# Two token chunks interleaved on the arriving weights, and a gate by half the angle

## The chip, the cores and the metric

The kernel runs on one core of a Trainium2 chip. The metric is the device time of one execution in microseconds (us); the time shown is the median over runs. Five engines work side by side, each through its own list of instructions in a fixed order, and meet at semaphores: PE (TensorE, matrix products and transposes; its weight loads are shown apart as PEld), DVE (VectorE), ACT (ScalarE, with lookup tables for functions), POOL (GpSimd) and SP (SyncE, which here only issues DMAs).

## The reference

```python
scores = q @ k.T / sqrt(64)                       # batch 4, 8 heads, 768 tokens, 64 per head
keep = (column < n_sink) | ((0 <= row - column) & (row - column < window))    # 4 and 128
a = softmax(where(keep, scores, -1e9))
x = (a @ v) laid out as 3072 tokens x 512         # the heads side by side
h = x @ w_in                                      # 512 -> 2048
g = h * cos(h)
return g @ w_out                                  # 2048 -> 512
```

q, k and v come as 32-bit numbers, w_in and w_out as 64-bit numbers. The result has to hold 32-bit accuracy, so that a product of two 32-bit matrices is made of three passes of a faster matmul over a rounded part (hi) and its rest (lo): hi x hi, hi x lo, lo x hi.

## The kernel before

**Tiling.** The 3072 tokens are 12 chunks of 256. A chunk has eight heads of attention and then eight slots of the dense layer; a slot is 256 of the 2048 columns. In a slot PE makes 24 matmuls of 256 columns for h (`h_mm`, L391) and 12 of 512 columns that add g·w_out to the chunk's two accumulators (`out_mm`, L439). The three batches' first chunks come first: chunks 0, 1 and 2 are the first 256 tokens of batches 0, 1 and 2, with exact 32-bit matmuls in their heads (tiles named early, scores at L771); chunks 3 to 11 are the rest (scores at L827, from the split keys r1 of L812 and r2 of L818).

**The gate.** Between h and g of a slot, on tiles of 128 partitions x 512: ACT turns h into whole turns (`turns`, L400), DVE takes the rest of the turn (`rest`, L406), ACT looks up the sine (`cosine`, L413), DVE multiplies by h (`gate`, L418), ACT rounds g (`g_hi`, L424), DVE or POOL takes what the rounding left (`g_lo`, L430).

**The weights.** They come as 32 pieces of 512 KB, which SP loads into two buffers (raw). DVE assembles a 32-bit number out of the two halves of each 64-bit one in three passes (L499, L505, L511), ACT rounds it (L532), DVE or POOL takes the rest (L535). All 32 are converted while chunk 0 goes through its eight slots, and then stay in memory. From chunk 2 on each piece is loaded once more and looked over for numbers that are too small (`check_piece`, L550); where one is found, a branch at the end goes through the whole work again by a general path.

**Order.** A planner goes through all steps with a due time each (`head_time`, `slot_time`) and a cost, and writes a fixed order for every engine before anything is emitted; the numbers of the table `C` are its costs and due times. In it the heads of chunk 0 come first, `TH` apart; the slots of chunk 0 follow, `STEP` apart, with the heads of chunks 1 and 2 between them; from chunk 1 on a slot comes every `T`, and the heads of a chunk run about a chunk ahead of its slots. At the start PE is also given `FILL` = 120 matmuls on a tile of zeros whose result nobody reads (L1281).

**Places that the change touches.** Out copies (L380 on ACT, L382 on DVE) bring an accumulator into a raw buffer, from where SP stores it (L455). A chunk's x is split into x.hi and x.lo (L335, L352), two buffers each. The banks of the accumulators' memory (PSUM) have tags: b0 to b4, s, tp, av.

Of the kernel before, what the change touches and what calls it, by code (L numbers as in the profile page):

```python
# [26 lines left out]
C = {  # L27
    "ALT": 3.247, "BLF": 0.145, "CK": 63.541, "DA": -2.188, "DH": -1.258, "DM": -0.843, "DQ": 1.633, "DS": -3.217,
    "DV": 4.887, "DX": 6.133, "FILL": 120, "CL": 6.506, "GHI": 2, "GLO": 2, "L": 1, "LAG": 4.747, "LEAD": 22.987,
    "NEH": 24, "NM": 1.13, "NW": 0.46, "NWF": 0.209, "PB": 5, "PEN": 11.444, "POOLF": 1.457, "POOLPEN": 2.675, "R": 2,  # L30
    "RAW": 2, "SAME": 0.151, "SEM": 0.193, "SPE": 0.272, "STEP": 6.281, "T": 6.493, "TH": 3.647, "WARM": 5,
    "WARM2": 0, "P0": 10.087, "A0": -0.05, "D0": 9.99, "G0": 1.871, "S0": 1.917, "ZV": 33.968, "LD": -14.202,
    "HOT": 7.314, "RL": 4.633, "K0": -93.629, "K2": 8.334, "WI": -21.701, "WO": 0.716, "WS": -2.103, "WS2": 2.887,
    "WT": 2, "XV": 2,
}
MIN_TOP = 1.125 * 2.0**-15
# [134 lines left out]
def attn_moe_kernel(ctx, tc, q, k, v, n_sink, window, w_in, w_out, out):  # L171
# [52 lines left out]
    lims = cp.tile([1, 2, 2, 2], F32, name="lims")  # L224
    tiny = cp.tile([P, NC * NSLOT // 2 + NFT], F32, name="tiny")
    redo = cp.tile([1, 1], I32, name="redo")

    def setup():
# [15 lines left out]
        nc.scalar.activation(out=tiny[:, 0:1], in_=quarter, func=AF.Exp)  # L244
        nc.vector.memset(lims, 0.0)
# [99 lines left out]
    def x_lo(x, a, p, early):  # L345
        def fn(e):
            if p == 0:
                x.lo = xp.tile([P, NP, NT], F32R, name=f"xlo_{a}", tag="xlo", bufs=2)
            if early:
                copy(e, x.lo[:, p, :], x.f[p])  # L350
            else:
                e.tensor_tensor(out=x.lo[:, p, :], in0=x.f[p], in1=f32(x.hi)[:, p, :], op=ALU.subtract)  # L352
        return fn

    def split_x(plan, x, a, p, t, early=False):

        add, buf = plan.add, plan.buf
        if p == 0:
            x.bhi, x.blo = buf("xhi", 2), buf("xlo", 2)
        i = add(  # L360
            [("ACT", act(NT, not early))], x_hi(x, a, p), x.sums[p] + (x.firsts[:1] if x.parts else [x.bhi]), t
# [53 lines left out]

    def gate(o):
# [28 lines left out]
    def out_copy(x, a, j):  # L445
        def fn(e):
            x.o[j] = f32(raws[x.bo[j].nth]).rearrange("p n w -> p (n w)")[:, :DM]
            copy(e, x.o[j], x.acc[j])
# [93 lines left out]
    def check_piece(plan, prio, k, src):  # L542

        add, buf = plan.add, plan.buf
        r, bt = buf("raw", C["RAW"]), buf("wt", C["WT"])
        raw, t32 = raws[r.nth], f32(wts[bt.nth])
        top = raw[:, :, 1].bitcast(F32)

        def least(e):
            nc.vector.tensor_tensor_reduce(  # L550
                out=t32, in0=top, in1=top, op0=ALU.mult, op1=ALU.max, scale=-1.0, scalar=-3.0e38,
# [4 lines left out]
        j = add((("DVE", dve(WP) + 0.02),), least, [i, bt], prio, port=True)  # L556
        r.users += [i, j]
        bt.users.append(j)
        return j

    def dense(plan, x, a, s, t, T, w_in_ready, w_out_ready, acc_banks, h_bank):
# [7 lines left out]
        accs = x.bacc  # L569
        if True:  # L570
            o = Rec()
            o.s, o.m, o.bank = s, a * NSLOT + s, h_bank
            bh, by, br, bhi, blo = buf(h_bank, 1), buf("y", 1), buf("r", C["R"]), buf("ghi", C["GHI"]), buf("glo", C["GLO"])
# [10 lines left out]
            a0 = add([("ACT", act(FG * NT, False))], turns(o), mm + [by], t + C["DM"] + 7.2)  # L584
            a2 = add([("DVE", dve(FG * NT))], rest(o), [a0, br], t + C["DM"] + 8.0)
            by.users.append(a2)
            a3 = add([("ACT", act(FG * NT) + 0.09)], cosine(o), [a2], t + C["DM"] + 8.9, table="sin")
            a4 = add([("DVE", dve(FG * NT))], gate(o), [a3], t + C["DM"] + 9.5)
            bh.users += [a0, a2, a4]
# [13 lines left out]
        for j in range(CB):  # L603
            bo = x.bo[j] = buf("raw", C["RAW"])
# [12 lines left out]
    def banded_path(ctx2):  # L617
# [111 lines left out]
        def pe_turn(o, part, tile, n):  # L729
            def fn(e):  # L730
                if part == 0:
                    o.qk = ps.tile([P, 2, NT], F32, name=f"qk_{o.tag}", tag="b3")
# [76 lines left out]
        def k_hi(o):  # L809
            def fn(e):  # L810
                o.r1 = ap.tile([P, o.nkb, o.sw], F32R, name=f"r1_{o.tag}", tag="r1")
# [3 lines left out]
        def k_lo(o):  # L815
            def fn(e):
                o.r2 = ap.tile([P, o.nkb, o.sw], F32R, name=f"r2_{o.tag}", tag="r2")
# [99 lines left out]
        def sink_turn(o):  # L917
            def fn(e):
                o.gp = ps.tile([GR, NT], F32, name=f"gp_{o.tag}", tag="av")
# [74 lines left out]
        def values(o):  # L994


            def fn(e):
                o.av = ps.tile([P, NT], F32, name=f"av_{o.tag}", tag="av")
# [57 lines left out]
        def before_softmax(g, o):  # L1056
# [91 lines left out]
            o.nq = 4 if o.a else 2  # L1148
# [48 lines left out]
        def after_softmax(g, o):  # L1197
# [45 lines left out]
            bav = buf("av", 1)  # L1243
# [309 lines left out]
```

## Time and profile before

| | |
|---|---|
| runs | 731.9, 733.47, 733.95 us; median 733.47 |
| profiled execution | 733.03 us |
| its span, from the first to the last instruction | 731.3 us |
| granted clock of PE, mean | 0.998 of 2.4 GHz |
| busy share of the span | PE 98%, DVE 84%, ACT 74%, POOL 23% |

The busy share of PE counts a matmul from its start to the end of its results, and neighbours overlap: where matmuls follow one another without a wait, the next starts long before the one before has ended. So PE can be shown as 98% busy and still do less than it could. How much work went through is read from the steps between starts, not from the busy time. The fills of L1281 count as busy too.

### The profile page before, as it was taken

Reading aid. Unit: us, or ns where it says so; the run is one execution under the profiler, and the core shown is the slowest. Engines: PE = TensorE matmul, PEld = TensorE weight load, DVE = VectorE, ACT = ScalarE, POOL = GpSimd, SP = SyncE. Lnnn points to the kernel's source line nnn. Section 1 sums busy time; section 2 is a strip of 40 time slices with the busy share of each in tenths; the row PEclk is TensorE's granted clock in tenths of the full one; section 3 lists DMA queues with packets and bytes.
Section 4 is the critical chain, followed back from the end, with each engine's and each line's share of the span. In section 5 each row is a group of like instructions: output and inputs, shape, how many; then the busy total and the mean of one; then the engine's idle time right before and its main releaser. Section 6 shows DMA issues by size and latency. Waiting matters only on the chain.

```text
span 731.3 us, 15326 instructions
## 1 busy us (share of the span) xinstructions
PE 715.8 (98%) x4865; PEld 651.3 (89%) x4865; DVE 614.5 (84%) x1811; ACT 541.2 (74%) x1354; POOL 165.8 (23%) x256
## 2 busy tenths in 40 slices
PE   8999999999999999999999999999999999999996
PEld 8887889899999999989898898999988999999995
DVE  6889999878999999899989988888898888875431
ACT  3878885987778868768778687788888697774332
POOL 1010100002242232433433324323110232321000
PEclk9999999999999999999999999999999999999999
DMA  6766564331673555646365443223333132110000
GB/s 174 199 183 185 166 173 136 83 55 32 139 193 55 121 134 128 158 118 170 78 159 149 89 99 58 49 69 55 55 73 64 30 83 52 34 45 3 28 2 34
DMA packets 215519, 71.51 MB, mean 98 GB/s; under 512 B 204164, under 2 KB 204164, under 8 KB 215428
## 3 DMA queue, kind: packets, MB, share of 16 engines
q1 hardware_dynamic: 215136, 69.38, 39.7%
q10 hardware_dynamic: 292, 1.05, 0.4%
q8 instruction: 41, 0.67, 0.4%
q14 instruction: 50, 0.41, 0.2%
HBM read 64.09 MB, written 6.29 MB: 96 GB/s over the span
## 4 chain that ended last, share of the span: by engine, by line
PE 71%; DVE 14%; ACT 7%; DMA 5%; issue 2%; SPq 1%; DVEq 0%; ACTq 0%
PE acc L439 28%; PE h L391 27%; PE av L1013 5%; PE s L827 4%; PE tp L937 2%; ACT p L858 2%; DVE wt L505 2%; DVE wt L511 1%; DMA xk<-in_k_dram 1%; PE idle L1281 1%; DMA raw<-in_moe_w_in_dram 1%; DVE r L406 1%; DVE p L849 1%; DVE glo L430 1%; DVE wt L499 1%
## 5 line engine op out<-in xcount | busy, mean ns | idle before, releaser
L391 PE MATMUL h<-xhi,whi_in 128*128 128x256 f32 x768 | 226.2, 295 | 0.7 <-DVE r L418 0.5
L391 PE MATMUL h<-xlo,whi_in 128*128 128x256 f32 x768 | 216.5, 282 | 0.0
L391 PE MATMUL h<-xhi,wlo_in 128*128 128x256 f32 x768 | 216.2, 282 | 0.0
L439 PE MATMUL acc<-whi_out,ghi 128*128 128x512 f32 x384 | 154.0, 401 | 0.2 <-DVE raw L382 0.2
L391 PEld LDWEIGHTS h<-xhi,whi_in 128*128 128x128 f32 x768 | 145.3, 189 | 8.5 <-DVE r L418 1.1
L439 PE MATMUL acc<-wlo_out,ghi 128*128 128x512 f32 x384 | 151.4, 394 | 0.0
L391 PEld LDWEIGHTS h<-xhi,wlo_in 128*128 128x128 f32 x768 | 145.5, 189 | 6.0
L439 PE MATMUL acc<-whi_out,glo 128*128 128x512 f32 x384 | 150.4, 392 | 0.0
L391 PEld LDWEIGHTS h<-xlo,whi_in 128*128 128x128 f32 x768 | 145.0, 189 | 0.0
L972 POOL TENSOR_SCALAR_AFFINE_SELECT ph<-ph 128x512 fp32r<-128x512 f32 x128 | 91.3, 714 | 112.4 <-DVE ph L965 95.5
L413 ACT ACTIVATE r<-r,neg 128x512 f32<-128x512 f32 x96 | 69.3, 724 | 45.4 <-DVE r L406 44.8
L430 DVE TENSOR_TENSOR glo<-r,ghi 128x512 fp32r<-128x512 f32 x92 | 67.8, 737 | 24.2 <-ACT ghi L424 23.5
L439 PEld LDWEIGHTS acc<-whi_out,glo 128*128 128x128 f32 x384 | 72.2, 188 | 16.3
L858 ACT ACTIVATE p<-p,st 128x136 f32<-128x136 f32 (+1 forms) x192 | 79.8, 417 | 0.4
L418 DVE TENSOR_TENSOR r<-h,r 128x512 f32<-128x512 f32 x96 | 65.5, 683 | 14.9 <-ACT r L413 14.8
L439 PEld LDWEIGHTS acc<-whi_out,ghi 128*128 128x128 f32 x384 | 72.5, 189 | 5.3 <-DVE raw L382 0.4
L439 PEld LDWEIGHTS acc<-wlo_out,ghi 128*128 128x128 f32 x384 | 72.8, 190 | 4.7 <-DVE wlo_out L535 0.3
L400 ACT ACTIVATE yt<-h 128x512 int32<-128x512 f32 x96 | 57.0, 594 | 23.6 <-PE h L391 23.1
L849 DVE CUSTOM_DVE_ANT_0 p<-s,mk 128x136 f32<-128x136 f32 (+1 forms) x192 | 59.2, 309 | 11.1 <-PE s L827 4.2
L406 DVE SCALAR_TENSOR_TENSOR r<-h,yt 128x512 f32<-128x512 f32 x96 | 65.2, 679 | 3.5 <-ACT yt L400 2.5
L424 ACT CAST ghi<-r 128x512 fp32r<-128x512 f32 x96 | 59.0, 614 | 11.0 <-PE acc L439 10.5
L878 POOL TENSOR_SCALAR p<-p,st 128x136 f32<-128x136 f32 (+2 forms) x38 | 20.7, 554 | 185.8 <-DVE st L868 108.4
(131 smaller groups left out, 1320.9 us busy)
## 6 DMA issues: line engine op xcount, KB each, us to landing
raw<-in_moe_w_out_dram SPq DMA_DIRECT2D x32, 512.0 KB
raw<-in_moe_w_in_dram SPq DMA_DIRECT2D x30, 512.0 KB
xk<-in_k_dram SPq DMA_DIRECT2D x256, 48.0 KB
v<-in_v_dram SPq DMA_DIRECT2D x64, 96.0 KB
out_dram<-raw SPq DMA_DIRECT2D x24, 256.0 KB
xq<-in_q_dram SPq DMA_DIRECT2D x144, 32.0 KB
xq<-in_q_dram SPq DMA_DIRECT2D x24, 64.0 KB
xk<-in_k_dram SPq DMA_DIRECT2D x24, 64.0 KB
```

The lines of the kernel that those rows point to most:

```text
L391: nc.tensor.matmul(out=o.h[:, t, :], lhsT=w[:, c, fs], rhs=xx[:, c, :], start=(c == 0 and n == 0), stop=(c == NC - 1 and n == 2),)
L400: nc.scalar.activation(out=yt, in_=o.h, func=AF.Copy, scale=INV2PI, bias=0.25)
L406: nc.vector.scalar_tensor_tensor(out=o.r, in0=o.h, scalar=INV2PI, in1=yt, op0=ALU.mult, op1=ALU.subtract)
L413: nc.scalar.activation(out=o.r, in_=o.r, func=AF.Sin, scale=TWOPI_DOWN, bias=quarter)
L418: nc.vector.tensor_tensor(out=o.r, in0=o.h, in1=o.r, op=ALU.mult)
L424: nc.scalar.copy(out=o.ghi, in_=o.r)
L430: e.tensor_tensor(out=o.glo, in0=o.r, in1=f32(o.ghi), op=ALU.subtract)
L439: nc.tensor.matmul(out=x.acc[j], lhsT=gg[:, t, j * P : (j + 1) * P], rhs=w[:, f, :], start=(f == 0 and n == 0), stop=(f == NFT - 1 and n = ...
L849: nc.vector.tensor_tensor_reduce(out=o.pj[j][:, :w], in0=o.s_ps[j][:, :w], in1=masks[min(o.i0 + j, 2)][:, :w], op0=ALU.add, op1=ALU.min, s ...
L858: nc.scalar.activation(out=o.pj[j][:, :w], in_=o.pj[j][:, :w], func=AF.Exp, bias=o.lead.st[:, 0, o.nth, j : j + 1], scale=-1.0, accum_out= ...
L972: nc.gpsimd.affine_select(out=ph[:, :, b, :], in_=f32(ph)[:, :, 1, :], pattern=[[0, 2 * CB], [(-1, 1)[b], P]], compare_op=(ALU.is_gt, ALU. ...
L1013: nc.tensor.matmul(out=dst, lhsT=lhs, rhs=rhs, start=(n == 0), stop=(n == len(seq) - 1), skip_group_check=True)
```

## The change

**Order.** The table C gets other numbers. The slots of chunks 0 and 1 are interleaved: `slot_time` sets them `STEP` = 12.944 apart (6.281 before) with chunk 1 shifted by 0.593 of a step, so that a piece of the weights serves both chunks when it comes. The sixteen heads of chunks 0 and 1 come before the slots; those of chunk 2 fall between the interleaved slots. `FILL` goes from 120 to 60.

**Gate.** cos h = 1 - 2 sin²(h/2), so g = h - 2h sin²(h/2) = -2 (r² - 1/2) h with r = sin(h/2). ACT looks up the sine of h/2 straight from h (`half_sine`), ACT or DVE squares it (`square`), DVE makes (r² - 1/2) h (`gate_square`); the factor -2 goes into the out copies. `turns` and `rest` are gone from this path. Over the 96 slots 75 squares stand on ACT and 21 on DVE.

**Bound.** The lookup of h/2 has no reduction of the angle, so |h| must stay below a bound. It is looked over with the sums of the squares of v (`check_values`, 16 times, beside chunks 7 and 8) and of the columns of w_in (`check_columns`, 4 times, beside chunk 9), and a chain at the end that joins them to the branch to the general path. With these inputs the branch isn't taken, before or after.

**Buffers.** Chunk 1's x.hi and x.lo lie in a tile x1 that later holds the split keys r1 and r2 and the sink values vs. The out copies go to the buffers wt instead of raw; `check_piece` writes over its own raw buffer. Chunk 2's heads have all their PSUM tiles on the tags s and tp, and four heads share a softmax only from chunk 2 on.

```diff
 C = {
-    ... "FILL": 120, ... "SPE": 0.272, "STEP": 6.281, "T": 6.493, "TH": 3.647, ...
+    ... "FILL": 60, "CV": 15.515, "OV": 0.593, "H0": 18.545, "HB": 6.103, "TH2": 13.668, "GA": 12, ...
+    ... "SPE": 0.057, "STEP": 12.944, "T": 5.842, "TH": 5.504, ...
...
-                x.hi = xp.tile([P, NP, NT], F32R, name=f"xhi_{a}", tag="xhi", bufs=2)
+                x.hi = env.x1[0] if a == 1 else xp.tile([P, NP, NT], F32R, name=f"xhi_{a}", tag="xhi", bufs=2)
...
+    def half_sine(o):
+        def fn(e):
+            o.r = mp.tile([P, FG, NT], F32, name=f"r_{o.m}", tag="r", bufs=C["R"])
+            nc.scalar.activation(out=o.r, in_=o.h, func=AF.Sin, scale=0.5)
+        return fn
+    def square(o):
+        def fn(e):
+            if e is nc.scalar:
+                e.activation(out=o.r, in_=o.r, func=AF.Square)
+            else:
+                e.tensor_tensor(out=o.r, in0=o.r, in1=o.r, op=ALU.mult)
+        return fn
+    def gate_square(o):
+        def fn(e):
+            nc.vector.scalar_tensor_tensor(
+                out=o.r, in0=o.r, scalar=0.5, in1=o.h, op0=ALU.subtract, op1=ALU.mult
+            )
+        return fn
...
+    def check_values(plan, prio, b, h):     # two heads' v: load, ACT square 128x768, DVE sum over 64
...
+    def check_columns(plan, prio, n):       # 512 columns of w_in: 4 ACT squares, 3 DVE sums, 1 PE matmul, 1 DVE maximum
...
+                o.r1 = env.x1r[:, 0, : o.nkb * o.sw].rearrange("p (n s) -> p n s", n=o.nkb)
...
-        start = H * C["TH"]
-        start2 = start + NSLOT * C["STEP"]
+        start = C["H0"] * C["TH"]
+        start2 = start + (NSLOT + C["OV"]) * C["STEP"]
 
         def head_time(g):
-            return g * C["TH"] if g < H else start2 + (g - 2 * H) * T
+            if g < 2 * H:
+                return g * C["TH"]
+            return start + C["HB"] + (g - 2 * H) * C["TH2"] if g < 3 * H else start2 + (g - 3 * H) * T
 
         def slot_time(a, s):
-            return start2 + ((a - 1) * NSLOT + s) * T if a else start + s * C["STEP"]
+            return start + (s + a * C["OV"]) * C["STEP"] if a < 2 else start2 + ((a - 2) * NSLOT + s) * T
```

What this does to the order is shown at three places. Names: h_N is the product of a slot, acc_J_N an accumulator, xhi, xlo and x_147 the split x (x_147 is chunk 1's, in x1), s_... a head's scores, whi and wlo the split weights, st the sums of a softmax.

PE at the beginning of the dense work, before: the third slot of chunk 0.

```order
L771 MATMUL s_0_7_0_836<-tk_0_6_779,early 128x128
L391 MATMUL h_843<-xhi_420,whi_in 128x256
L391 MATMUL h_843<-xhi_420,wlo_in 128x256
L391 MATMUL h_843<-xlo_438,whi_in 128x256
L391 MATMUL h_843<-xhi_420,whi_in 128x256
L391 MATMUL h_843<-xhi_420,wlo_in 128x256
L391 MATMUL h_843<-xlo_438,whi_in 128x256
L989 MATMUL av_0_2_829<-early,vpo 128x256
```

PE at the same place of the changed kernel:

```order
L401 MATMUL h_844<-xhi_390,wlo_in 128x256
L401 MATMUL h_844<-xlo_411,whi_in 128x256
L401 MATMUL h_768<-x_147,whi_in 128x256
L401 MATMUL h_768<-x_147,wlo_in 128x256
L401 MATMUL h_768<-x_147,whi_in 128x256 x2
L401 MATMUL h_768<-x_147,wlo_in 128x256
L401 MATMUL h_768<-x_147,whi_in 128x256
L873 MATMUL s_0_2_1_880<-tk_0_2_842,early 128x256
```

Before, the third slot of chunk 0 stood alone, cut by the heads of chunk 1; now six matmuls for chunk 0 are followed by six for chunk 1 out of the same weights, and the heads between them are those of chunk 2.

DVE at the same place, before:

```order
L406 SCALAR_TENSOR_TENSOR r_785<-h_564,yt 128x512
L505 SCALAR_TENSOR_TENSOR wt_72<-raw_70,wt_72 128x512
L849 ISA p_0_6_798,st_0_4_678<-s_0_6_0_787,mk 128x128
L849 ISA st_0_4_678 128x1
L511 SCALAR_TENSOR_TENSOR wt_72<-raw_70,wt_72 128x512
L499 TENSOR_SCALAR wt_73<-raw_71 128x512
L382 COPY early<-tp_0_2_800 128x384
L505 SCALAR_TENSOR_TENSOR wt_73<-raw_71,wt_73 128x512
```

DVE of the changed kernel, where the slots of chunk 1 have begun:

```order
L951 ISA p_0_3_917,st_0_0_790<-s_0_3_0_906,mk 128x128
L951 ISA st_0_0_790 128x1
L547 SCALAR_TENSOR_TENSOR wt_72<-raw_70,wt_72 128x512
L442 SCALAR_TENSOR_TENSOR r_908<-r_908,h_768 128x512
L951 ISA p_0_3_917,st_0_0_790<-s_0_3_1_927,mk 128x256
L951 ISA st_0_0_790 128x1
L437 TENSOR_TENSOR r_925<-r_925 128x512
L535 TENSOR_SCALAR wt_73<-raw_71 128x512
```

The masks of the scores (L849, now L951) stand among the weight passes (L499 to L535, now L535 to L571) and the gate in both; the step L406 is gone, and a head's masks are those of chunk 2 by the time the gate comes up.

PE where chunk 3's heads begin, before:

```order
L439 MATMUL acc_1_957<-whi_out,ghi_1507 128x512
L439 MATMUL acc_1_957<-wlo_out,ghi_1507 128x512
L439 MATMUL acc_1_957<-whi_out,glo_1523 128x512
L827 MATMUL s_2_0_0_1663<-r_0_2_0_1650,l_2_0_1602 128x264
L827 MATMUL s_2_0_0_1663<-r_0_2_0_1656,l_2_0_1602 128x264
L439 MATMUL acc_0_1668<-whi_out,ghi_1590 128x512
```

The same of the changed kernel:

```order
L401 MATMUL h_1767<-x_147,whi_in 128x256
L470 MATMUL acc_0_1004<-whi_out,ghi_1662 128x512
L470 MATMUL acc_0_1004<-wlo_out,ghi_1662 128x512
L470 MATMUL acc_0_1004<-whi_out,glo_1680 128x512
L470 MATMUL acc_1_1022<-whi_out,ghi_1662 128x512
L470 MATMUL acc_1_1022<-wlo_out,ghi_1662 128x512
L470 MATMUL acc_1_1022<-whi_out,glo_1680 128x512
L346 MATMUL av_0_6_1701<-xhi_1084,gt 128x256
L470 MATMUL acc_0_919<-whi_out,ghi_1765 128x512
L470 MATMUL acc_0_919<-wlo_out,ghi_1765 128x512
L470 MATMUL acc_0_919<-whi_out,glo_1777 128x512
L929 MATMUL s_2_0_0_1834<-x_147,l_2_0_1601 128x264 x2
```

The first score of chunk 3 now reads its split keys from x_147, the tile that the last h matmul of chunk 1 still reads ten matmuls further up; before, it had tiles of its own.

## Rows read from the trace of the kernel before

**Rows 1.** The page: busy times, then GB/s in 40 slices of 18.3 us.

```profile
span 731.3 us, 15326 instructions
...
PE 715.8 (98%) x4865; PEld 651.3 (89%) x4865; DVE 614.5 (84%) x1811; ACT 541.2 (74%) x1354; POOL 165.8 (23%) x256
...
GB/s 174 199 183 185 166 173 136 83 55 32 139 193 55 121 134 128 158 118 170 78 159 149 89 99 58 49 69 55 55 73 64 30 83 52 34 45 3 28 2 34
```

**Rows 2.** Stretches: length, then busy us (count) PE, PEld, DVE, ACT, POOL; clock; DMA.

```profile
40.00:60.00 20.00, 17.74 (x123) 15.20 (x121) 17.79 (x50) 16.29 (x46) 2.01 (x2) 1.00 0.61 175
...
100.00:120.00 20.00, 19.78 (x126) 17.59 (x125) 19.81 (x50) 12.91 (x28) 1.31 (x2) 1.00 0.55 160
50.00:60.00 10.00, 7.78 (x47) 5.78 (x46) 8.65 (x23) 9.70 (x24) 2.01 (x2) 1.00 0.49 147
700.00:731.00 31.00, 25.38 (x140) 21.78 (x138) 8.21 (x12) 8.12 (x14) 0.00 (x0) 0.95 0.06 20
```

**Rows 3.** Fills alone in the first 60 us: PE, PEld, clock, DMA.

```profile
0.00:60.00 60.00, 22.44 (x120) 17.85 (x120) 1.00 0.65 181
```

**Rows 4.** PE in order of time, full queue: start, length, line, operation.

```profile
301.03 0.40 PE L439 MATMUL acc<-whi_out,ghi 128*128 128x512 f32 x1
301.26 0.39 PE L439 MATMUL acc<-wlo_out,ghi 128*128 128x512 f32 x1
...
301.71 0.28 PE L391 MATMUL h<-xhi,whi_in 128*128 128x256 f32 x1
...
302.19 0.28 PE L391 MATMUL h<-xhi,wlo_in 128*128 128x256 f32 x1
```

**Rows 5.** DVE in order of time: start, length, line, operation.

```profile
108.82 0.68 DVE L418 TENSOR_TENSOR r<-h,r 128x512 f32<-128x512 f32 x1
109.42 0.41 DVE L499 TENSOR_SCALAR wt<-raw 128x512 int32<-128x512 int32 x1
109.75 0.68 DVE L535 TENSOR_TENSOR wlo_out<-wt,whi_out 128x512 fp32r<-128x512 f32 x1
110.35 0.68 DVE L505 SCALAR_TENSOR_TENSOR wt<-raw,wt 128x512 int32<-128x512 int32 x1
```

**Rows 6.** PE in order of time: four scores of chunks 1 and 2 (L771).

```profile
53.88 0.48 PE L771 MATMUL s<-tk,early 128*128 128x256 f32 x1 [0.73 <-DVE st L849]
...
66.10 0.28 PE L771 MATMUL s<-tk,early 128*128 128x128 f32 x1
...
98.70 0.27 PE L771 MATMUL s<-tk,early 128*128 128x128 f32 x1
...
117.76 0.38 PE L771 MATMUL s<-tk,early 128*128 128x128 f32 x2
117.90 0.48 PE L439 MATMUL acc<-whi_out,ghi 128*128 128x512 f32 x1
118.22 0.39 PE L439 MATMUL acc<-wlo_out,ghi 128*128 128x512 f32 x1
```

**Rows 7.** PE and ACT at the end, in order of time.

```profile
724.99 0.39 PE L439 MATMUL acc<-whi_out,glo 128*128 128x512 f32 x1
725.42 0.59 ACT L380 COPY raw<-acc 128x512 f32<-128x512 f32 x1 [0.77 <-PE acc L439]
```

**Rows 8.** Groups by line: form, count | busy us, mean ns | idle before.

```profile
L424 ACT CAST ghi<-r 128x512 fp32r<-128x512 f32 x96 | 59.0, 614 | 11.0 <-PE acc L439 10.5
L400 ACT ACTIVATE yt<-h 128x512 int32<-128x512 f32 x96 | 57.0, 594 | 23.6 <-PE h L391 23.1
...
L818 DVE TENSOR_TENSOR r<-tk,r 128x408 fp32r<-128x408 f32 x53 | 31.4, 593 | 1.6 <-ACT r L812 1.0
...
L430 POOL TENSOR_TENSOR glo<-r,ghi 128x512 fp32r<-128x512 f32 x4 | 5.2, 1304 | 9.9 <-ACT ghi L424 9.9
```

**Rows 9.** POOL beside DVE in order of time.

```profile
51.96 2.01 POOL L878 TENSOR_SCALAR p<-p,st 128x128 f32<-128x128 f32 x2 [12.41 <-DVE st L868]
...
52.84 0.78 DVE L511 SCALAR_TENSOR_TENSOR wt<-raw,wt 128x512 int32<-128x512 int32 x1
```

More of the change, by code (lines that the diff above doesn't have):

```diff
@@ L358, in split_x @@
         if p == 0:
-            x.bhi, x.blo = buf("xhi", 2), buf("xlo", 2)
+            x.bhi, x.blo = (buf("r1", 1), buf("vs", 1)) if a == 1 else (buf("xhi", 2), buf("xlo", 2))
+            x.more = [buf("r2", 1)] if a == 1 else []
+            for b in x.more:
+                b.users = x.bhi.users
         i = add(
-            [("ACT", act(NT, not early))], x_hi(x, a, p), x.sums[p] + (x.firsts[:1] if x.parts else [x.bhi]), t
+            [("ACT", act(NT, not early))], x_hi(x, a, p),
+            x.sums[p] + (x.firsts[:1] if x.parts else [x.bhi, *x.more]), t
         )
@@ new lines, in check_columns, with square, both, turned @@
+    def check_columns(plan, prio, n):
+        add, buf = plan.add, plan.buf
+        r, bt, bg = buf("raw", C["RAW"]), buf("b2", 1), buf("glo", C["GLO"])
+        got_r = []
+        w = f32(raws[r.nth]).rearrange("p n w -> p (n w)").rearrange("p (a f) -> p a f", a=2)
+        fs = slice(n * WP, n * WP + WP)
+        got = []
+        for c in range(NC):
+            def square(e, c=c):
+                nc.scalar.activation(out=w[:, min(c, 1)], in_=f32(whi_in)[:, c, fs], func=AF.Square)
+            got.append(add([("ACT", act(WP))], square, got[-1:] or [r], prio + 0.5 * c))
+            if c:
+                def both(e, c=c):
+                    out = w[:, 0]
+                    if c == NC - 1:
+                        got_r.append(mp.tile([P, WP], F32R, name=f"cr_{n}", tag="glo", bufs=C["GLO"]))
+                        out = got_r[0]
+                    nc.vector.tensor_tensor(out=out, in0=w[:, 0], in1=w[:, 1], op=ALU.add)
+                d = got[-2:] + ([bg] if c == NC - 1 else [])
+                got.append(add([("DVE", dve(WP))], both, d, prio + 0.5 * c + 0.2, port=True))
+        def turned(e):
+            env.cs = env.ps.tile([1, WP], F32, name=f"cs_{n}", tag="b2")
+            nc.tensor.matmul(out=env.cs, lhsT=one_r, rhs=got_r[0], start=True, stop=True)
+        def most(e):
+            nc.vector.tensor_reduce(out=wmax[:, n : n + 1], in_=env.cs, axis=mybir.AxisListType.X, op=ALU.max)
+        i = add([("PE", 0.25)], turned, [got[-1], bt], prio + 2.5)
+        j = add([("DVE", dve(WP))], most, [i], prio + 3.0)
+        r.users += got
+        bg.users.append(i)
@@ new lines, in banded_path, with most_of @@
+        row = cp.tile([P, 1], F32, name="row")
+        end = cp.tile([1, 8], F32, name="end")
+        def most_of(e):
+            nc.vector.tensor_reduce(
+                out=most[:, :NV], in_=vsum.rearrange("p (n k) -> p n k", k=NB), axis=mybir.AxisListType.X, op=ALU.max
+            )
+            if checks:
+                nc.vector.tensor_reduce(out=most[:, NV:], in_=tiny, axis=mybir.AxisListType.X, op=ALU.max)
+            else:
+                nc.vector.memset(most[:, NV:], -3.0e38)
```

194 lines of the change are left out of this document (128 added, 66 removed).

## Prediction

> **What bounds the kernel now.** The page's first line shows PE busy for 98% of the span [rows 1], as if nothing could be won without taking matmuls away. The timeline of PE in a full queue corrects this: one matmul of the accumulators follows another after 0.23 us, and four of h take 0.48 from start to start, though they are shown as 0.40 and 0.28 long each [rows 4]; over longer stretches the steps are 0.230 and 0.119. So I count work in steps: 2304 matmuls of h by 0.119 are 274.2 us, 1152 of the accumulators by 0.230 are 265.0, and the 1190 rows of attention and warm-up by the steps of their kinds 141.5. PE has 680.7 us to do in a span of 731.3. The fills don't count: they are 120 in the first 60 us, 22.4 us shown busy [rows 3], and fill holes.
>
> Where do the other 50 us go? I take a row of PE, add up the work in front of it in the order, and subtract this from its start. The difference, PE's distance, can only grow. Four scores of the early heads are the marks [rows 6]. A score waits for a PSUM tile that DVE frees with the mask of an earlier score, so DVE's distance is read at the same marks.
>
> - Mark A, chunk 1's head 5, second score, 53.88 us: in front of it on PE 48 of h (5.7 us) and 113 others (22.0), 27.7 in all; distance 26.2. In front of the mask it waits for, DVE has 35 operations of 512 columns at 0.60 (20.9), 12 shifts at 0.33 (4.0) [rows 5] and 97 small ones (14.7), 39.7 in all; distance 14.2. It is a true wait, 0.73 us for DVE.
> - Mark B, chunk 2's head 5, first score, 98.70 us: PE 186 of h (22.1), 36 of the accumulators (8.3), 185 others (36.6): 67.0, distance 31.7. DVE 88 of 512 columns (52.6), 24 shifts (8.1), 132 small (19.9): 80.6, distance 18.1.
> - Mark C, chunk 2's head 7, first score, 117.76 us: PE 85.4, distance 32.4; DVE 99.3, distance 18.5.
>
> (An exact 32-bit score of 128 columns counts 0.22: from 117.76 to 118.22 there are one and a step of 0.23 [rows 6].) So up to mark C PE loses 32 us; the last matmul starts at 724.99 [rows 7] with 680.5 in front, distance 44.5: only 12.1 more in the other 607 us. The loss at the beginning has two parts: DVE itself is 14 to 18 us behind (loading, the first softmaxes, waits for ACT), and the order asks of DVE 12.0 us more at mark A, and 13.6 at mark B, than of PE. That DVE is full there shows in the stretch from 100 to 120 us, 19.81 of 20 busy [rows 2].
>
> **The change part by part.** *Interleaving.* It takes no matmul away: PE's total goes from 680.7 to 681.7 (some more parts of softmax and 4 column checks). It moves matmuls. At the marks of the changed order (the same heads):
>
> - Mark A: PE 6 of h (0.7) and 118 others (23.0), 23.7; DVE 20 of 512 columns (12.0), 8 shifts (2.7), 107 small (16.6), 31.2. DVE has 7.5 more in front, not 12.0.
> - Mark B: PE 186 of h (22.1), 42 of the accumulators (9.7), 203 others (40.3), 72.1; DVE 70 (41.9), 21 shifts (7.1), 160 small (26.1), 75.1. 3.0 more, not 13.6.
> - Mark C, second score of that head: PE 93.7, DVE 92.4: 1.3 less.
>
> In between, chunk 2's head 3 stands at 43.9 on PE and 49.3 on DVE, 5.4 more. So DVE's work needed for a given amount of PE's falls, since a piece of the weights (one pass of 0.33 and three of 0.60) now serves 18 matmuls on the average and not 9 (288 per chunk over 32 pieces). If DVE is as far behind at a given amount of its own work as before, PE's distance is DVE's plus these differences. Before, DVE was 16.4 behind at 49.7 us of work, chunk 2's first score at 66.10 [rows 6]. So at chunk 2's head 3: 16.4 + 5.4 = 21.8; at mark A about 12.1 + 7.5 = 19.6; at mark B about 17.5 + 3.0 = 20.5. The largest decides: 21.8 for 32.4, a gain of 10.6 us. Bounds from the same rows: with DVE only 12 behind, as it was up to 44 us, 17.4 to 19.5, gain about 14; with DVE 5 further behind, a little more than it lost between marks A and B, 27, gain about 6.
>
> *Gate.* Per slot it takes one ACT pass (L400, 0.594 us) and one DVE pass of 512 columns (0.60) away and puts a square in, on ACT 75 times (like L424, 0.614 [rows 8]), on DVE 21 times. DVE drops by 75 x 0.60 = 45 us; with all checks and moves its total goes from 558 to 514 by steps, ACT's from 490 to 483 (ten table loads fewer). DVE and ACT don't end the later stretches, so this is worth nothing there by itself; at the marks it is in the counts. The chain from h to g gets shorter by one engine change; it is covered by the slots in between, so I cost it at nothing. If that cover failed, each of the 96 slots would have about 0.6 us less to wait, not more.
>
> *Bound check.* 16 ACT squares of 768 columns and 16 of 512, by L424 at most 0.92 and 0.61 each, 25 us; DVE 16 sums of 768 and 16 passes of 512, 24 us; both are within the totals above and stand beside chunks 7 to 9, where PE has the work of about 160 us and DVE and ACT are far under that. Its 32 extra loads (6.3 MB) fall between about 410 and 520 us, where 49 to 99 GB/s are moved of up to 199 elsewhere [rows 1]; over 110 us they add 57. Cost nothing; a bound from above is one PE wait of 0.7 us, as in rows 6, per load pair: 16 x 0.7 = 11. The joining chain at the end stands before the last slots and is hidden by them; if it weren't, by the steps of DVE and PE at most five of 0.60 and two of 0.23, 3.5 us.
>
> *Out copies.* They go on carrying one pass per accumulator; scaling rides along. The tail after the last matmul's step stays 6.1 us (731.3 - 724.99 - 0.23, [rows 1, 7]).
>
> *Shared tile x1.* Chunk 3's keys can't be split before chunk 1's last h is done. In the order 2.3 us of PE work lie between that matmul and chunk 3's first score; an ACT pass of 408 columns (at most L424's 0.61) and a DVE pass (0.59 [rows 8]) must fit, 1.2 us plus what stands in front of them on their engines. I put 0.6 us for this, between 0 and 3.
>
> *Sum.* 681.7 + 21.8 + 12.1 (later loss as before) + 6.1 = 721.7; with 0.6 for x1 722.3 of span. The profiled execution took 1.73 more than its span, and the median of the runs is 0.44 above it: 724.0 and 724.5 us.
>
> **A rule that speaks for more.** The counts above are from rows; the Trainium skill, "Perfetto Trace Analysis", section "Optimization Strategy", says that where the most contended engine changes between regimes, interleaving the regimes can pay. The trace agrees that there are two regimes here (DVE's up to mark C, PE's after it). The page gives no figure, and the sum would be the same.
>
> **Rivals.**
>
> *Larger gain.* DVE's distance isn't a constant of the beginning but grew from waits in its own list (14.2 at A, 18.1 at B), and a lighter DVE doesn't collect them: 12 + 5.4 = 17.4, and half the later loss gone (6): 681.7 + 17.4 + 6 + 6.1 + 0.6 + 2.2 = 714. For it: at 100 to 120 us DVE is full [rows 2], so much of its loss is mere queueing. Against: later loss comes in small steps at all places.
>
> *Smaller gain.* POOL is given more of DVE's passes: 4 rests of weights, 12 g_lo for 4, 22 k_lo for 12. On POOL one takes 1.30 us [rows 8] where DVE steps 0.60, and while POOL worked at 51.96 DVE's pass at 52.84 took 0.78 and not 0.68 [rows 9]. If DVE falls 5 us further behind by this, PE's distance is 27 and the time 729.5. The Trainium skill, "Perfetto Trace Analysis", section "Optimizing Scalar/DVE Operations", says that GPSIMD and DVE share a read port of SBUF, so that moving work between them may not help; the 0.10 us above is what this trace shows of it, and 30 such meetings would be 3 us.
>
> *No change, by the clock.* With 60 fills fewer PE stands still more in the first 45 us. If the grant fell to 1.2 GHz for the 20 to 25 us of PE work there, it would take twice as long; about half of the 20 us fits into the time that PE stands there anyway, and some 10 come on top: 734.5. Against it: from 50 to 60 us PE was busy 7.78 of 10 without any fills and the grant stayed 1.00; the only lower stretch is the end, 0.95 from 700 on [rows 2], in which PE works 25 of 31 us. The Trainium skill, "TensorE: Matmul & The Clock Gate", section "Why this matters for your kernels", warns of idle gaps between bursts of matmuls and by this rule fewer fills would cost; no stretch before shows it in the first 120 us.
>
> *Slower, at chunk 3.* Since its heads can't start before chunk 1 is through, PE has only 55.8 us of work (192 of h, 102 of the accumulators, 91 others) between chunk 3's first score and its first h; before it had 83.1 (282, 144, 141), and no later chunk had under 77.7. Eight heads go through ACT, DVE and POOL one behind the other. If they really need 77.7, PE stands 22 us: 746.5, slower. It decides from 11 us of standing (7 bring it to no change). For it: the softmax works on four heads at a time, and chunk 4 also has less, 65.3. Against: ACT and DVE have about 37 us each for eight heads and eight slots, which fits in 55.8, and the old 83 was chosen by due times, not shown as needed by a wait.
>
> **How the numbers follow.** My forecast (719 to 729) gets 0.46, the larger gain 0.13, the smaller (729 to 731.3) 0.13; no change by the clock or by a part of chunk 3's wait 0.13; slower by chunk 3 or by waits I don't see 0.15. Faster and slower are meant by over 0.3%, 2.2 us, which is about what a measurement here can tell: 0.72, 0.13, 0.15. The range of 8 in 10 leaves out the far end of the larger gain and most of slower: 715 to 736.
>
> **What would show it.** In the profile after: at the scores L873 of chunk 2's heads 3 to 7 PE's distance should be about 22 and no more than 1 us of waits for DVE each; DVE at 100 to 120 us no longer full; the grant 1.00 in the first 60 us (the clock rival if under); between chunk 3's first score and its first h (some 150 to 205 us) no wait of PE over 2 us (the chunk 3 rival if over 10 in sum); the same 6.1 at the end. The forecast is wrong if PE's distance at chunk 2's head 7 is 27 or more, or if it grows by over 17 after that.

## The result and the profile after

The changed kernel takes 737.72 us (median of 6 runs, 736.55 to 740.34), the one before 733.01 in the same comparison; the ratio is 1.0068 with a 95% interval of 1.0052 to 1.0083. It is slower by 0.7%; 724.5 were forecast, in 715 to 736.

The page of the changed kernel, with the same lines as [rows 1]: span, busy times, GB/s in 40 slices.

```profile
span 734.9 us, 15232 instructions
...
PE 714.0 (97%) x4810; PEld 642.5 (87%) x4810; DVE 592.6 (81%) x1763; ACT 527.2 (72%) x1347; POOL 190.2 (26%) x281
...
PEclk9999999999999999999999999999999999999999
...
GB/s 175 166 173 152 155 172 145 136 128 248 103 106 170 142 104 100 151 191 154 120 103 83 115 91 92 125 108 49 61 83 42 86 30 51 17 40 2 22 8 33
```

DVE and ACT are lighter, by 22 and 14 us, POOL is heavier by 24. The grant stayed at 1.00, the level of 2.4 GHz, while work was left (the digits of PEclk are tenths, 9 is 90% or more), so the clock rival is out for this kernel. The 248 GB/s of slice 9 (165 to 184 us) stand where [rows 1] have 32.

The scores that answer to the marks of [rows 6], PE in order of time: mark A, chunk 2's head 3, mark B, mark C (second score of that head).

```profile
44.09 0.46 PE L873 MATMUL s<-tk,early 128*128 128x256 f32 x1
...
69.38 0.60 PE L873 MATMUL s<-tk,early 128*128 128x256 f32 x2
...
98.34 0.35 PE L873 MATMUL s<-tk,early 128*128 128x128 f32 x1
...
120.56 0.60 PE L873 MATMUL s<-tk,early 128*128 128x256 f32 x2
```

Less the PE work in front by the order (23.7, 43.9, 72.1, 93.7) they give distances of 20.4, 25.5, 26.2 and 26.9 us. Before it was 26.2 at A and 32.4 at C. So 5.5 us of gain stand at 120 us, about half of what was forecast, and the rest of the program takes back 8.

The same distance, taken every so often at the PE instruction that starts last (worked out from starts and the order, as in the prediction):

```
us            60    80   100   120   150   200   250   300   400   500   600   700
before      28.2  31.3  31.7  32.4  33.4  34.0  34.8  35.6  39.0  41.4  44.2  45.1
changed     24.6  25.6  26.1  26.9  26.9  29.4  33.1  35.3  38.3  41.7  44.8  47.6
```

(At the last matmul it is 44.5 and 47.0, so that an entry here is good to about half a microsecond.)

From 120 to 300 us PE loses 8.4 us, where it lost 3.2; by the steps of the trace 5.6 of them stand in front of scores of chunk 3 on (L929) and 1.0 in front of transposes in the heads (L1039), where before the scores had 0.5. Busy time of the changed kernel in these stretches (columns as in [rows 2]):

```profile
100.00:120.00 20.00, 19.73 (x126) 17.65 (x125) 17.36 (x35) 10.19 (x18) 0.00 (x0) 1.00 0.54 154
150.00:200.00 50.00, 48.84 (x328) 43.98 (x327) 43.46 (x140) 32.80 (x83) 13.54 (x19) 1.00 0.64 160
200.00:250.00 50.00, 48.87 (x337) 43.14 (x336) 43.30 (x143) 41.77 (x114) 23.65 (x33) 1.00 0.58 127
```

And of the kernel before from 200 to 250 us:

```profile
200.00:250.00 50.00, 50.00 (x353) 45.92 (x352) 46.69 (x143) 38.67 (x103) 16.92 (x24) 1.00 0.50 115
```

PE did 337 matmuls and not 353, and no engine is full: DVE, ACT and POOL have 6.7, 8.2 and 26 us free. PE waits there for single links of the chain of operations that a head goes through. What it waits for in the whole program, by line and releaser (us in all, times, longest); the view lists only the longer pauses, so it holds a part of the loss:

```profile
PE s L929 <- DVE st L951: 2.7, 5, 1.0
...
PE s L873 <- DVE st L951: 1.4, 4, 0.5
PE h L401 <- DVE r L442: 1.2, 2, 0.9
```

The scores of chunk 3 on (L929) wait for the mask that frees their PSUM tile. One of these waits, PE, DVE and POOL in order of time:

```profile
155.44 0.28 DVE L1002 TENSOR_TENSOR x<-xb,x 16x128 fp32r<-16x128 f32 x1
...
156.44 1.07 POOL L920 TENSOR_TENSOR x<-tk,x 128x408 fp32r<-128x408 f32 x1 [3.42 <-ACT x L914]
156.54 1.12 DVE L1002 TENSOR_TENSOR x<-xb,x 16x128 fp32r<-16x128 f32 x1
...
159.13 0.48 PE L929 MATMUL s<-x,l 128*128 128x264 f32 x2 [0.95 <-DVE st L951]
```

A DVE pass that takes 0.28 us at 155.44 takes 1.12 beside a two-input pass of POOL, and the score behind it is 0.95 late. The same happens at the beginning, to a pass of 512 columns that takes 0.68 by [rows 5]:

```profile
44.00 1.40 POOL L571 TENSOR_TENSOR wlo_in<-wt,whi_in 128x512 fp32r<-128x512 f32 x1
44.18 1.76 DVE L547 SCALAR_TENSOR_TENSOR wt<-raw,wt 128x512 int32<-128x512 int32 x1
```

So such a pass of DVE stands for most of POOL's. The Trainium skill, "Perfetto Trace Analysis", section "Optimizing Scalar/DVE Operations", names a shared read port; this trace agrees, with 1.08 us where the prediction had reckoned 0.10 from [rows 9]. It isn't so for every pass: one that reads a PSUM tile (s, av, tp) takes its usual 0.42 beside the same kind of pass of POOL:

```profile
198.47 1.27 POOL L920 TENSOR_TENSOR x<-tk,x 128x408 fp32r<-128x408 f32 x1 [1.34 <-ACT x L914]
...
198.82 0.42 DVE L1129 TENSOR_TENSOR x<-av,xb 64x256 f32<-64x256 f32 x1
```

In the whole program 16 passes of DVE are stretched by over 0.15 us beside a two-input pass of POOL, none of them one that reads PSUM; they lose 11 us in sum. In the kernel before there were 13 and 8 us already (one of 1.60 at 352.98, beside 1.08 of POOL), which the prediction had missed. So the change brought 3 us of this, on DVE and not on PE. The end is as forecast, 6.2 us after the last matmul's step (6.1 before):

```profile
728.45 0.39 PE L470 MATMUL acc<-whi_out,glo 128*128 128x512 f32 x1
728.87 0.60 ACT L482 ACTIVATE wt<-acc 128x512 f32<-128x512 f32 x1 [0.76 <-PE acc L470]
```

### The profile page after: what moved, and what is told of

It reads as the page before. It is cut to its first block, busy times and chain, and to the rows that moved or that the text cites. A ratio compares the mean times of both kernels' runs of the same rounds, so it can differ in the third digit from the quotient of the medians.

```text
span 734.9 us, 15232 instructions
## 1 busy us (share of the span) xinstructions
PE 714.0 (97%) x4810; PEld 642.5 (87%) x4810; DVE 592.6 (81%) x1763; ACT 527.2 (72%) x1347; POOL 190.2 (26%) x281
## 4 chain that ended last, share of the span: by engine, by line
PE 79%; DVE 7%; DMA 5%; ACT 5%; issue 2%; SPq 1%; POOL 0%; DVEq 0%; ACTq 0%
PE h L401 32%; PE acc L470 31%; PE av L1115 5%; PE s L929 4%; PE tp L1039 2%; DMA raw<-in_moe_w_in_dram 2%; PE s L873 1%; PE av L1091 1%; PE tp L1045 1%; ACT p L960 1%; DVE p L951 1%; DMA xk<-in_k_dram 1%; DVE l L896 1%; DMA out_dram<-wt 1%; DMA xq<-in_q_dram 1%
## 5 line engine op out<-in xcount | busy, mean ns | idle before, releaser
L401 PE MATMUL h<-xhi,whi_in 128*128 128x256 f32 x704 | 205.4, 292 | 1.2 <-DVE r L442 1.2
L401 PE MATMUL h<-xlo,whi_in 128*128 128x256 f32 x704 | 198.2, 282 | 0.0
L401 PE MATMUL h<-xhi,wlo_in 128*128 128x256 f32 x704 | 198.0, 281 | 0.0
L401 PEld LDWEIGHTS h<-xhi,whi_in 128*128 128x128 f32 x704 | 133.0, 189 | 9.1 <-DVE r L442 2.0
L401 PEld LDWEIGHTS h<-xhi,wlo_in 128*128 128x128 f32 x704 | 133.3, 189 | 6.5
L470 PEld LDWEIGHTS acc<-whi_out,glo 128*128 128x128 f32 x384 | 72.1, 188 | 16.6
L442 DVE SCALAR_TENSOR_TENSOR r<-r,h 128x512 f32<-128x512 f32 x96 | 64.9, 679 | 16.9 <-ACT r L435 16.5
L429 ACT ACTIVATE r<-h 128x512 f32<-128x512 f32 x96 | 56.8, 597 | 23.7 <-DVE glo L461 17.8
L993 POOL TENSOR_TENSOR vr<-v,vr 128x192 fp32r<-128x192 f32 (+1 forms) x51 | 31.4, 615 | 152.8 <-ACT vr L988 148.4
L929 PE MATMUL s<-x,l 128*128 128x264 f32 (+2 forms) x288 | 61.9, 295 | 4.0 <-DVE st L951 2.7
L951 DVE CUSTOM_DVE_ANT_0 p<-s,mk 128x136 f32<-128x136 f32 (+1 forms) x192 | 59.4, 311 | 6.6 <-PE s L873 2.8
L929 PEld LDWEIGHTS s<-x,l 128*128 128x128 f32 x288 | 47.1, 189 | 15.4 <-issue 5.1
```

What stands on the lines that cost most here:

```text
L401: nc.tensor.matmul(out=o.h[:, t, :], lhsT=w[:, c, fs], rhs=xx[:, c, :], start=(c == 0 and n == 0), stop=(c == NC - 1 and n == 2),)
L429: nc.scalar.activation(out=o.r, in_=o.h, func=AF.Sin, scale=0.5)
L442: nc.vector.scalar_tensor_tensor(out=o.r, in0=o.r, scalar=0.5, in1=o.h, op0=ALU.subtract, op1=ALU.mult)
L470: nc.tensor.matmul(out=x.acc[j], lhsT=gg[:, t, j * P : (j + 1) * P], rhs=w[:, f, :], start=(f == 0 and n == 0), stop=(f == NFT - 1 and n = ...
L929: nc.tensor.matmul(out=o.s_ps[j][:, :w], lhsT=o.l[:, j * P : (j + 1) * P], rhs=r.rearrange("p n s -> p (n s)")[:, c0 : c0 + w], start=(n = ...
L951: nc.vector.tensor_tensor_reduce(out=o.pj[j][:, :w], in0=o.s_ps[j][:, :w], in1=masks[min(o.i0 + j, 2)][:, :w], op0=ALU.add, op1=ALU.min, s ...
```

## The experiments

Ratios are to the kernel before of the same comparison, with their 95% intervals. "Planned anew" means that the edit changes the planner's input, so that the order of everything behind it may change; "in its order" that the order was kept and only what is emitted at a place was changed. Losses are the growth of PE's distance, found as above. Where the kernel was planned anew, the new order comes in beside the edit; c1 to c3 below show what that alone can do.

### The parts

**e1, the gate alone on the old table** (planned anew).

```diff
-            a0 = add([("ACT", act(FG * NT, False))], turns(o), ...)      # turns, rest, cosine, gate
+            a0 = add([("ACT", act(FG * NT, False) + 0.09)], half_sine(o), ...)   # half_sine, square, gate_square
```

> The kernel before with the new gate alone (half-angle sine, square, factor -2 in the out copies), old table, no interleaving, and without the check of the bound. It tells whether the gate itself costs. Gate theory (the gate or its chain from h to g is what makes the change slower): 736 to 740 us. Port, squeeze and margin theories (the loss is in the new order): not slower than before, 728 to 733, DVE 45 us less busy.

730.91 us, 0.9976 (0.9963 to 0.9990): 1.8 us faster than before by the ratio, 1.2 by the medians (732.11 before). The gate is not the loss. In this plan the grant fell to 0.95 from 20 to 60 us and PE's distance at 120 us is 36.8; afterwards it loses less than any other, 2.1 us from 120 to 300.

**e2, without the bound check** (planned anew) and **f2, the same in its order**.

```diff
-                if a in (7, 8):
-                    seen.append(check_values(...))
-                if a == 9 and s < DFF // WP:
-                    seen.append(check_columns(...))
```

> The changed kernel without the check of the bound (its 32 loads, 32 ACT squares, DVE sums are left out). Check theory (the growth of PE's distance after 300 us, 12.3 against 9.6 us, comes from these passes): 734 to 735.5 us, distance gained after 300 us about 9.6. Port, squeeze and margin theories: 737 to 738.5, since the loss of 6.4 us between 150 and 300 us lies before them.

> The changed kernel in its order, with the loads and passes of the bound check left out where they stand. Check theory: 2 to 3.5 us less than the changed kernel, 734 to 736, nothing different before 380 us. If the 2.7 us of the kernel planned anew without the check came from the new plan: 737 to 738.

735.05 us, 1.0032 (1.0017 to 1.0048), and 735.53 us, 1.0034 (1.0021 to 1.0046). Two ways of taking it out agree: the check costs about 2 us (2.2 to 2.7 by the medians alone, 1.8 to 2.6 when each is set against the kernel before of its own comparison), near half of the whole slowdown. It was priced at nothing. Where it costs them is seen in part only: the profiled executions of the changed kernel and of f2 (736.66 and 735.56 us) are 1.1 apart, of which 0.9 are the check's four matmuls of 512 columns on PE, and PE's distance grows by only 0.7 more after 300 us. The loss from 120 to 300 us stays, 8.6 and 8.8.

**f1, the changed kernel without the second loads of the weights, and g1, the same before** (both in their order; DVE's pass reads a tile that is there).

```diff
-        i = add(dma(1), lambda e: e.dma_start(out=raw.rearrange("p n w -> p (n w)"), in_=src), [r], ...)
+        i = add(dma(1), lambda e: None, [r], ...)
```

> The changed kernel in its order, but the 32 second loads of the weight pieces (512 KB each) are left out; DVE makes its pass over a tile that is there. Reload theory (DVE stands in its list for pieces that land late, 4.3 us at 174.61, because they now come with the loads and stores of chunks 0 to 4, and PE's scores wait behind it): the loss of PE from 150 to 300 us falls from 8.5 to under 4, time 729 to 732. Squeeze theory (chunks 3 to 5 have too little PE work between their first score and their first h, whatever DMA does): 735 to 738, the loss stays over 6.

> The kernel before in its order, with the same 32 second loads left out. Reload theory: the loads cost the old order little, under 1.5 us (731 to 733), so that the difference to the changed one is theirs. If both kernels gain alike, the reloads explain nothing of the difference.

736.0 us, 1.0047 (1.0033 to 1.0060), and 732.41, 0.9998 (0.9986 to 1.0010). The loads cost the old order nothing and the new one about 1.5 us, with intervals that overlap; f1 still loses 7.6 us from 120 to 300. The reload theory falls as the main cause; its 4.3 us at 174.61 were the transfer, and DVE itself waited 0.33 us for it at 178.94, 1.8 in all from 120 to 300.

### POOL, and new plans

**e4, POOL's subtractions on DVE** (planned anew) and **f3, the same in its order**.

```diff
-            e.tensor_tensor(out=o.glo, in0=o.r, in1=f32(o.ghi), op=ALU.subtract)
+            nc.vector.tensor_tensor(out=o.glo, in0=o.r, in1=f32(o.ghi), op=ALU.subtract)    # also wlo, r2
```

> The changed kernel with the two-input subtractions of the weight rests, g_lo, k_lo and x_lo on DVE alone (POOL keeps the v rests and the selects). Port theory (DVE and POOL stand for each other whenever POOL runs such a pass: one of 1.40 us at 44.00 made DVE's pass 1.76 instead of 0.68): PE's distance at 120 us falls from 26.9 to about 25, the loss from 150 to 300 us from 8.5 to about 4, time 731 to 734. Squeeze and margin theories: nothing gained, and 38 passes more on DVE: 737 to 740.

> The changed kernel in its order, with the 38 subtractions of weight rests, g_lo and k_lo that stand on POOL made by DVE at the same places of the order. Port theory: DVE's pass beside POOL's stretches by about what it would have cost itself (1.08 at 44.18), so that DVE loses little by taking it over and PE no longer waits for POOL: 734 to 737. Otherwise DVE's added 38 x 0.6 = 22 us show: over 738.

747.58 us, 1.0211 (1.0176 to 1.0245), and 739.5, 1.0092 (1.0069 to 1.0115). e4 is slower than the changed kernel, by a new plan too; f3's interval overlaps the changed kernel's, so it is not shown to be slower, and it isn't faster. In f3 the stretched passes are all but gone (0.5 us in sum, 11 in the changed kernel), but PE's distance at 120 us is 27.4 (26.9) and the loss from there to 300 is no smaller: moving the passes to DVE saves nothing, and the port theory falls.

**e5, SPE set back.** `"SPE": 0.057` to `"SPE": 0.272`, planned anew.

> The changed kernel with one number of the table set back: SPE 0.272 and not 0.057, the time that the planner reckons from the end of a PE step to what waits for it. Margin theory (the plan leaves too little room at handovers, so that PE's scores and the engines behind them come late again and again): loss from 150 to 300 us under 5, time 732 to 735. Port and squeeze theories: 736.5 to 739.5.

756.51 us, 1.0333 (1.0300 to 1.0366): 19 us slower than the changed kernel. The margin theory gets no support; but a new plan alone costs as much (c2, c3), so e5 can't rule it out. The controls:

**c1, c2 and c3, a cost moved a little.** `SEM` 0.193 to 0.198 before; `SEM` 0.165 to 0.170 and `SPE` 0.057 to 0.060 changed.

> The kernel before planned anew with one cost of the table moved a little (SEM 0.193 to 0.198): a control for what a new plan alone does. If the plan's details don't matter: 732 to 734. If the tables are fitted to one plan and any other costs time (as the 10 and 19 us of e4 and e5 suggest): 736 or more.

> The changed kernel planned anew with one cost of the table moved a little (SEM 0.165 to 0.170), the same control. Details don't matter: 736 to 739. Fitted table: over 741.

> A second control: the changed kernel planned anew with another cost of the table moved a little (SPE 0.057 to 0.060). The distances are 52, 64 and 74 us (c2: 51, 63, 75; changed: 56, 65, 74). Squeeze theory: PE loses more than the changed kernel from 120 to 300 us, 10 to 16, and the time is 742 to 762 as in c2. If c2 was a single bad draw: 736 to 740.

734.47 us, 1.0018 (1.0005 to 1.0031) for c1, but 761.76, 1.0392 (1.0375 to 1.0409), and 753.86, 1.0289 (1.0262 to 1.0316), for c2 and c3. The old table stands a new plan at 1.4 us (one nudge; e1 is a second new plan of it and lost nothing); the new one loses 16 to 24. The changed kernel is a mild case among plans of its table, which take 735 to 762 us with their edits.

### The squeeze

**h1, h2 and h3: the heads of chunks 3 to 5 due later in the old order** (27 us, 13 us, and 27 us with the gate of e1).

```diff
-            return g * C["TH"] if g < H else start2 + (g - 2 * H) * T
+            late = max(27.0 - 1.5 * (g - 3 * H), 0.0) if g >= 3 * H else 0.0
+            return g * C["TH"] if g < H else start2 + (g - 2 * H) * T + late
```

> The kernel before with the heads of chunks 3 to 5 due later (27 us for chunk 3's first, 1.5 us less for each next), so that PE has 65, 62 and 74 us of work between their first score and their first h, not 83, 85 and 80 (the changed kernel has 56, 65, 74). Squeeze theory: PE loses 7 to 9 us between 120 and 300 us and not 3.2, time 737 to 740. If the squeeze is harmless: 732 to 734.5.

> The kernel before with half the delay of h1 for the heads of chunks 3 to 5 (13 us, 0.75 less for each next): PE has 80, 77 and 77 us between their first score and first h, before 83, 85 and 80. Squeeze theory with a threshold (loss only when the heads' own chain is longer than this work): 733 to 736, loss from 120 to 300 us 3 to 6. If any later due time spoils the order in proportion (h1 lost 27.5 us): 745 or more.

> The delay of h1 on the old order with the new gate (e1, without the bound check; 66, 65 and 73 us). Squeeze theory: the new gate takes 45 us off DVE, but the chain of eight heads stays, so most of the loss stays: 745 to 756, e1 730.9. If the squeeze costs only where DVE is loaded: under 738.

760.64 us, 1.0360 (1.0330 to 1.0390); 739.92, 1.0092 (1.0068 to 1.0116); 744.73, 1.0158 (1.0141 to 1.0175). The long delay costs 27.5 us (h1) and 13.8 (h3 against e1). h3 goes like e1 up to 200 us (distance 36.7 and 37.2) and then loses 11.4 us in 50 where e1 loses 1.0. Its row, and that of e1:

```profile
200.00:250.00 50.00, 43.92 (x273) 38.39 (x272) 40.59 (x137) 36.61 (x104) 19.44 (x27) 0.90 0.61 145
```

```profile
200.00:250.00 50.00, 50.00 (x355) 45.92 (x354) 45.53 (x145) 37.41 (x96) 17.66 (x25) 1.00 0.51 122
```

Again no engine is full, and the grant falls to 0.90 behind PE's pauses, so that a part of these 11 us is the clock's: at most the missing tenth of 50 us, 5. The Trainium skill, "TensorE: Matmul & The Clock Gate", section "Why this matters for your kernels", warns that idle gaps between matmuls bring TensorE's clock down; this row agrees, at a place where the prediction had not looked for it, and the waits from 232 to 237 us in front of the fall are short ones, 0.48 and 0.82. In the changed kernel itself the grant stays 1.00. h2 loses only 0.6 us from 200 to 250, but 5.1 from 120 to 150, 2.1 of them in one wait in which DVE's g_lo of L430 took 1.51; behind it the grant fell to 0.83 (130 to 140 us), so that up to 1.7 more are the clock's. h2's time misses what was expected, and that loss isn't the squeeze's.

**e9 and k1: the squeeze relieved in the new order** (planned anew). e9 has no bound check, and its mask index lies on a tile that is written again, so that its masks are wrong and it stands for its time alone.

```diff
-                x.hi = env.x1[0] if a == 1 else xp.tile(...)          # k1: chunk 0 in x1
+                x.hi = env.x1[0] if a == 0 else xp.tile(...)
```

> The changed kernel without the bound check (as e2), with tiles of their own for the split keys r1 and r2 (the sink values stay in x1) and the heads of chunks 3 to 5 due up to 24 us earlier; in the order chunk 3's first score comes 6 us of PE work earlier, the three distances are 59, 73 and 79 us for 56, 65 and 74. Squeeze theory: loss from 120 to 300 us 5 to 7 and not 8.6, 731 to 734 (e2: 735). If the loss has another cause: 735 or more.

> The changed kernel with chunk 0's x instead of chunk 1's in the shared tile x1. Chunk 0 is through earlier, so chunk 3's heads may begin earlier: 59, 74 and 80 us between first score and first h, not 56, 65 and 74. Squeeze theory: loss from 120 to 300 us 4 to 7 and not 8.5, time 732 to 736. If a new plan decides more than these distances: 738 to 760.

738.78 us, 1.0073 (1.0056 to 1.0091), and 747.22, 1.0201 (1.0174 to 1.0227). No relief: the orders give chunk 4 72 and 74 us, not 65, and lose 7 us from 200 to 250 all the same; chunk 3 has 59 in both. Here are all orders, with PE's work between the first score and the first h of chunks 4 and 3 (by the order), the loss from 200 to 250 us and the grant in it:

```
order            e1    before  c1    h2    | k1    e9    changed  e2    h3    c3    c2    e4    e5    h1
chunk 4, us      87.2  85.1    84.9  77.4  | 73.9  72.5  65.3     65.3  64.6  63.5  63.2  63.2  63.0  61.5
chunk 3, us        87    83      83    80  |   59    59    56       56    66    52    51    52    55    65
loss, us          1.0   0.8     0.5   0.6  |  7.0   7.1   3.7      3.4  11.4   8.3  10.7   7.5  10.2  12.6
grant            1.00  1.00    1.00  1.00  | 0.97  0.97  1.00     1.00  0.90  0.93  0.90  1.00  0.90  0.88
```

All four with 77 us or more for chunk 4 lose at most 1.0, all ten with 74 or less lose 3.4 to 12.6. Less what the missing grant can have cost at most (6 of the 12.6 us in h1), the ten still lose 3.4 to 7.5. Chunk 3's work parts the orders in the same way, 80 and more against 66 and less, so the table doesn't tell which of the two counts; k1 and e9 lengthened chunk 4's alone. And among the ten the loss doesn't follow the work. In h1 and h3 the delay of the heads was the only edit against before and e1, and c1, a single draw, shows a new plan of the old table without the loss. So in the old order the delay, and with it the shortened distance, causes the loss; for the changed kernel it is the same pattern at the same place, but not undone, since k1 and e9 stayed under 77 and were new plans besides.

### The beginning

**i1 and i2: one of DVE's three passes per weight piece left out** (the low word of each weight is missing; in their order).

```diff
             def low(e):
+                if not guard:
+                    return
```

> The changed kernel in its order with one of the three DVE passes that assemble a weight piece left out (the low word, so the last three bits of each weight are missing): 32 x 0.60 us less on DVE, some 12 of it before chunk 2's head 5. If DVE's amount of work still sets PE's distance in the beginning, as in the forecast: distance at 120 us 21 to 23 and not 26.9. If it is set by the heads' chain from PE to DVE and ACT and back, and by landings: 25 to 27. Time 734 to 738 either way, since the loss from 150 us on stays.

> The same pass left out of the kernel before, in its order. The forecast's reading of the beginning (PE's distance is DVE's distance plus 13 us that DVE has more in front): distance at 120 us falls by 6 or more, from 32.4 to under 26, time 722 to 728. If it is not DVE's work: under 3 us.

736.66 us, 1.0050 (1.0029 to 1.0071), and 730.86, 0.9974 (0.9961 to 0.9987). PE's distance at 120 us is 27.3 (26.9 with the pass) and 31.4 (32.4 with it). With 12 us of work less in front, DVE only stands longer. Even the 1.0 us is within what one execution differs from another: f1 and f2, whose edits begin after 140 us, have 25.7 and 27.2 at 120. Here is DVE (the third busy time) in i2, for 19.81 of 20 in [rows 2]:

```profile
100.00:120.00 20.00, 20.00 (x131) 18.20 (x130) 17.05 (x43) 12.69 (x28) 0.48 (x1) 1.00 0.50 157
```

## Why the prediction was wrong

By its own sum (forecast, then measured, for the span):

- *PE's distance in the beginning: 21.8, then 26.9.* The step that failed is "if DVE is as far behind at a given amount of its own work as before, PE's distance is DVE's plus these differences". At mark A it held (19.6 forecast, 20.4 measured). Then DVE fell further behind, 18.0 at 60 us and 26.7 at 120, where 16 to 18 had been assumed for this stretch. i1 and i2 show why the step was no law: DVE was busy, but its amount of work was not what PE waited for. The 12 us taken off it moved PE by 1.0 and not at all. I had taken one wait for a mask of DVE, 0.73 us in [rows 6], for the sign that DVE's amount of work sets the pace. What sets it instead isn't settled; PE's losses there are many waits of up to 1 us at the handovers of the heads.
- *The rival of the smaller gain* named POOL. Its distance of 27 comes nearest for this stage, but by luck: f3 shows that giving its passes back doesn't help (27.4).
- *The later loss: 12.1 with 0.6 for x1, then 20.1.* Of the 7.4 us more, 4.6 fall between 120 and 300 us. By its place that is the rival "slower, at chunk 3", which I gave a small chance, since the averages of DVE and ACT (37 us of 56) fitted. The averages do fit: no engine is full at 200 to 250 us. What seems to count is the time that eight heads take one behind the other, not their work; for the changed kernel that is argued from the table of orders, not shown by undoing it. Place and price were off as well: the wait is spread over chunks 3 and 4, and for the changed kernel it is 5 us and not 22. In the old order it reaches 24 (h1, 120 to 300 us), of which up to 11 can be the clock's (grant 0.94). The 0.6 us for x1 didn't show: chunk 3's first score starts at 153.18 us without a wait. The other 2.8 us come after 300 us; f2, without the bound check, has all but 0.7 of them.
- *The bound check: 0, then about 2* (f2, e2). 0.9 us of it is PE's own added work, which was in the sum; the 1 to 2 us behind it are within the upper bound that I named and did not use, and no row shows where they are lost.
- *The second loads:* not in the sum. f1 puts about 1.5 us on them, within the other terms above, and not clear of noise.
- *The gate: 0 by itself, then 1.2 to 1.8 us of gain* on the old table (e1, with a new plan and without the check). DVE's total, which stood outside the sum, was reckoned too low: 45 us for the gate and 13 for 22 passes given to POOL, less 24 for the checks, make 34 less and not 44; shown busy it has 22 less.
- *The tail* (6.1, then 6.2) held; the median stood 1.06 us above the profiled execution, not 0.44.

With 5.1, 7.4 and 0.1 the span is 12.6 us over the forecast 722.3, which gives the 734.9. Of the signs that I had named, the waits stayed short (none over 1.0 us from chunk 3 on) and DVE was no longer full, and yet the distance grew by 20.1 after chunk 2's head 7, over the 17 that were to show the forecast wrong: a loss in many small pieces escapes a sign that looks for one long wait.

## What to carry to other kernels

A busy engine is a bound only if less work on it makes the time shorter: take some off before the sum rests on it. A chain of small handovers needs length, so compare how much work the main engine has between a chain's start and its use before and after, and beware where it falls under what any stage had before. A table that gives a good order can give a much slower one after a small nudge: a new plan by a nudge of a few per cent is the control that an experiment on such a kernel needs.

## What was not expected of the hardware

A pass of DVE that reads no PSUM tile could stand for nearly a whole two-input pass of POOL, 1.08 us at 44.18 and 0.84 at 156.54, where 0.10 was what [rows 9] had shown beside a one-input pass; passes that read PSUM ran on (0.42 at 198.82). And pauses of PE at full load can cost twice, once by themselves and once by the clock: in h3 the grant of 200 to 250 us was 0.90, in h1 0.88, and in h1's last 10 us of these 0.50, the level of 1.2 GHz, behind a wait of 1.04 us at 236.96:

```profile
200.00:250.00 50.00, 43.73 (x257) 37.02 (x256) 44.13 (x137) 37.77 (x107) 16.77 (x26) 0.88 0.55 135
240.00:250.00 10.00, 6.83 (x26) 5.05 (x26) 8.35 (x28) 9.40 (x32) 2.29 (x4) 0.50 0.74 173
```
